# The first MLP's first weight: its scale from TensorE products of its pieces instead of ScalarE squares, with a new stored sequence

## The chip, the core and the metric

The kernel runs on one core of one Trainium2 chip. The metric is device time in microseconds (us), lower is better. The core has five engines that run their own instruction queues side by side: TensorE (PE, matmuls; the loading of its stationary operand is listed apart as PEld), VectorE (DVE), ScalarE (ACT), GpSimd (POOL) and SyncE (SP, which here only issues DMAs). The tile framework makes an engine wait, by semaphores, where one instruction needs another's result or its buffer.

## What is computed

Windowed attention (4 batches, 8 heads, 576 positions, head size 64; plain windows for four heads and dilated ones for the other four), then two MLPs over the 2304 tokens. Cut to what matters:

```python
def _attn_ref(q, k, v):                      # 4 x 8 x 576 x 64
    scores = scale * np.matmul(q, k.transpose(0, 1, 3, 2))
    scores = np.where(masks[None], scores, -1000000000.0)   # window 32, or 32 steps of 4
    attn = softmax(scores)
    return np.matmul(attn, v)

def _moe_ref(x, w_in, w_out, g_ln):          # w_in 512 x 1024, w_out 1024 x 512
    h = x @ w_in
    solu = h * softmax(h)
    return (layernorm(solu) * g_ln) @ w_out

def _moe2_ref(x, w_in, w_out):               # 512 x 2048, 2048 x 512
    return softplus(x @ w_in) @ w_out
```

The large products are made in float16, each operand split into a high and a low half that are both scaled by a power of two. The scale of a weight is found on the chip, from the weight itself. The weights arrive as 8-byte floats.

## The kernel before

All work is cut into some 2900 named operations (`P.op`), each with one to a few dozen instructions. `Plan.order` (L92) does not decide anything: it walks the tuple `ORDER` (L191), which names the operations by their numbers in the sequence in which all engines get them, and takes each buffer from the slot that `SLOTS` names. A number above the count of operations means that DVE does an operation which ACT could do too. A negative number is a fill: a matmul of the 128x128 identity with four copies of itself, 512 columns, into a PSUM bank that is free just then; its result is never read. So the order on every engine is fixed beforehand, and every engine executes its own list strictly in that order.

`weights` (L708) prepares one weight. It is called for `w1i` (the first MLP's first weight, 8 pieces of 128x512), `w1o` (8 pieces), and for each quarter `w2i0` to `w2i3` and `w2o0` to `w2o3` of the second MLP's weights (4 pieces each). Per piece it makes:

- `w1i.3l`: the DMA that loads piece 3 (512 KB) into a raw buffer, of which there are four
- `w1i.3ca`, `cb`, `cc`: three DVE instructions that turn 8-byte floats into 4-byte ones
- `w1i.3s`: a Square on ACT over the 128x512 piece, with the sum of each row kept in a column of `amw`; the squares themselves are written over the raw buffer and never read
- after the squares of all pieces `w1im`, a product with a matrix of ones that sums `amw` over the partitions, and `w1iea` to `w1ied`, four small DVE instructions that make of the sum the power of two by which the weight is scaled
- `w1i.3h` and `w1i.3o`: the float16 high half (ACT or DVE) and low half (DVE)

The names of other operations: `pre0.6`, `pre0.6s` and `pre0m` (loads of a batch's q, k or v, their squares on ACT, the sum); for the pair of attention blocks `n`: `ldN` (loads), `tqN`/`tkN` (transposes on PE), `cqN`/`ckN` (copies out of PSUM), `QKN` (scores), `exN.0a`/`b` (largest entry on DVE, exponentials on ACT), `tpN`, `cpN` (the exponentials turned and copied), `PVN` (values), `nrN` (division), `txN`, `xhN`, `xlN` (the turned result and its two halves); from pair 10 on float16 pairs with `mx`, `ph`, `pl` and transposing DMAs `qT`, `kT`, `pT`. For tile `t` of 128 tokens `m1at`, `m1bt` are the products with `w1i`, and `m1mt` to `m1lt` its softmax and normalisation; `yaJ`, `ybJ` are the products with `w1o`, `hJ.p` and `oJ.p` those of the second MLP, `ghJ.p` and `glJ.p` its halves.

In the first third of the run all weights are prepared while attention and the first tiles go on; from some 237 us on the weights are done and PE works through the MLPs.

`weights` has a second way for the row sums, under the tuple `GRAM` of weight names (L186). It is empty in this kernel.

Of the kernel before, what the change touches and what calls it, by code (L numbers as in the profile page):

```python
# [13 lines left out]
ALU = mybir.AluOpType  # L14
AXX = mybir.AxisListType.X
# [129 lines left out]
def kernel(  # L145
# [12 lines left out]
    nc = tc.nc  # L158
# [27 lines left out]
    GRAM = ()  # L186
# [5 lines left out]
        64, 65, 237, -2, 240, 3166, 238, 268, -2, 242, 3168, -2, -2, 244, 245, 256, 267, 0, 270, 13, 14, 271, 257,  # L192
        3, 15, -2, -2, 272, 4, 66, 5, 67, 246, 16, -2, -2, -2, -2, -2, 247, 3173, 68, 6, 258, 69, -5, 70, 239, 273,
        -5, 274, 71, 72, 73, 74, 75, 269, 259, 275, 17, 1, 28, 7, 29, 286, 276, -5, 249, 298, 30, -5, -5, -5, -5,
        277, 2, 278, 250, 287, 18, 297, -5, -5, -5, -5, 303, 31, 304, 32, 260, 251, 288, 19, 3177, 253, 254, 20,
        21, 22, 261, 299, 300, 305, 306, 3214, 262, 33, -5, -5, -5, 279, 3188, 264, 255, 265, 280, 281, 34, 38,
        266, 35, 307, 308, 36, 282, 355, 283, 309, 290, 291, 23, 39, 292, -5, -5, -5, -5, -5, -5, 310, 40, 37, 284,
        24, 354, 41, 8, 25, 285, 26, 9, 353, 293, -5, -5, -5, -5, -5, 294, 311, 42, -5, 360, 352, 10, 11, 27, 295,
        296, 361, 319, 76, 12, 77, 301, 356, -5, -5, -5, -5, -5, -5, -5, -5, -5, -5, -5, -5, -5, -5, 43, 44, 45,
        46, 47, 358, 302, 320, 407, 91, -5, -5, -5, 321, 359, 408, 111, 78, 50, 362, 52, 2985, 322, 79, 62, 80, 53,  # L200
        363, 364, 312, 410, 437, 411, 313, 61, 374, 48, 92, 314, -5, -5, -5, -5, -5, -5, 365, 63, 323, 366, 3240,
        324, 49, 81, 93, 51, 375, -5, -5, -5, 316, 58, 412, 413, -5, 376, 377, 325, 357, 94, 106, 409, -5, -5, -5,
        -5, 414, 317, 326, 56, 95, 327, 328, 318, 59, 112, 415, 57, 113, 438, 329, 367, 107, 368, 114, 369, 416,
        54, 55, -5, -5, -5, -5, -5, -5, 417, 491, 1128, 418, -5, 440, 108, 426, 441, -5, 419, 96, 378, 109, 82,
        420, 379, 330, 83, 115, 380, 370, 371, 427, 492, 97, 110, 138, 84, 381, 372, 85, 428, 331, 98, 86, 489,
        373, 382, 99, 101, 429, 490, 100, 87, 421, 139, 442, 443, 422, 88, 332, 430, 431, 383, 89, 90, 102, 385,
        432, 333, 103, 384, 104, 227, 140, 545, 544, 439, 423, 497, 334, 495, 424, 335, 105, 496, 228, 172, 425,
        336, 433, 498, 141, 337, 142, 143, 386, 444, 149, 434, 467, 338, 339, 387, 211, 445, 154, 456, 435, 494,
        173, 340, 446, 174, 436, 848, 447, 175, 457, 341, 116, 150, 448, 342, 549, 176, 117, 144, 343, 847, 151,
        118, 344, 388, 119, 345, 152, 458, 547, 459, 346, 548, 449, 120, 450, 155, 550, 212, 347, 213, 493, 499,  # L210
        153, 156, 348, 500, 501, 157, 158, 451, -3, -3, -3, -3, -3, -3, -3, -3, -3, -3, 502, 121, 511, 512, 460,
        513, 503, 514, 850, 851, 3274, 3377, 350, 461, 145, 453, 462, 3047, 146, 454, 504, 463, 214, 852, 505, 464,
        455, 853, 225, 506, 3057, 3432, 147, 3049, 133, 177, -2, -2, -2, -2, 508, 226, 178, 148, 465, 466, 125,
        509, 510, 877, -4, -4, -4, -4, -4, -4, 159, 134, 126, 389, 878, 515, 516, 179, 517, 160, 3443, 180, 161,
        215, 551, 390, 552, 162, 392, 136, 216, 217, 163, 123, 553, -2, 519, 181, 182, 391, 563, 130, 520, 183, -2,
        -2, -2, -2, -2, -2, -2, -2, -2, 554, 521, 128, 555, 135, 468, 218, 522, 131, 564, 351, 219, 393, 184, 523,
        883, 129, 394, 137, 185, 395, 220, 186, 170, 565, 187, 164, 188, 880, 221, 546, 222, 127, 396, 189, 879,
        397, 190, 191, 566, 884, 398, 223, 171, 469, 574, 166, 224, 885, 399, 192, 849, 579, 854, 1129, 193, 229,
        165, 194, 400, 195, 168, 1124, 167, 401, 196, 230, 402, 1127, 886, 231, 169, 232, 855, 233, 403, 575, 234,
        576, 404, 235, 197, 577, 198, 866, -4, -4, -4, -4, -4, -4, -4, -4, -4, -4, 556, 470, 557, 405, 199, 1126,  # L220
        856, -4, 857, 578, 567, 568, 867, 580, 868, 558, 858, 859, 471, 569, 589, 559, 560, 581, 200, 860, 472,
        474, 473, 582, 869, 861, 406, 870, 1136, 201, 1137, 871, 590, 570, -5, -5, -5, 571, 475, 583, 202, 572,
        862, 591, 872, 573, 592, 524, 882, 584, -5, -5, -5, -5, 863, 203, 207, 204, 208, 593, 607, 864, 865, 585,
        205, 873, 938, 874, 881, 1170, 209, 875, 206, 586, 561, 562, 587, 476, 210, 477, 876, 939, 478, 608, 588,
        940, 479, 941, 609, 480, 1177, 610, -5, -5, 594, 481, 887, 888, 595, 482, 612, 596, 236, 483, 611, 597,
        484, 1178, 598, 889, 899, 613, 3524, 485, 900, 614, 617, 486, 3528, 615, 934, 525, 487, 935, 936, 890, 937,
        1125, 901, 616, 891, -5, -5, -5, -5, -5, 892, 618, 902, 601, 893, 903, 912, 619, 605, 1130, 942, 622, 894,
        895, 896, 602, 904, 1134, 620, 600, 621, 1132, 488, 526, 1131, 1133, 687, 623, 905, 624, 625, 1135, 1139,
        897, 898, 527, 1138, 606, 528, 626, 529, 943, 947, -5, -5, -5, 627, 628, 629, 682, 3869, 530, 630, 913,
        906, 631, 531, 1168, 945, 632, 633, 604, 634, 532, 910, 948, 635, 1169, 533, 907, 636, 908, 534, 637, 949,  # L230
        535, 1211, 644, 911, 909, 536, 640, 642, 638, 537, 914, 954, 959, 538, 645, 539, 915, 950, 639, 641, 643,
        540, 541, 542, 955, 688, 1171, 683, 689, 1140, 1172, 946, 690, 916, 1141, 684, 1142, 1175, 691, 1176, 1173,
        685, 917, 956, 543, 951, 919, 918, 672, 1154, 1143, 1209, 1180, 686, 957, 1174, 677, 1144, 1155, 1145, 920,
        953, 952, 673, 960, 1156, 921, 922, 1179, 674, 678, 675, 923, 679, 924, 1146, 1210, 680, 992, 1050, 1157,
        1051, 676, 1181, 925, 1182, 1212, 1158, 1159, 1214, 1052, 1183, 1213, 926, 710, 681, 961, 993, 994, 705,
        1216, 1195, 692, 693, 962, 694, 1184, 1215, 927, 695, 996, 1160, 696, 1217, 1273, 1220, 699, 1275, 1147,
        697, 1196, 1276, 701, 700, 997, 928, 1148, 1197, 958, 995, 963, 1149, 702, 703, 1185, 704, 1150, 1274,
        1161, 998, 929, 930, 1221, 1151, 698, 999, 1012, 706, 711, 1053, 707, 1222, 1152, 1153, 1198, 931, 1000,
        708, 1186, 932, 712, 709, 1283, 1054, 1162, 713, 714, 1284, 720, 965, 1187, 1013, 1223, 721, 1055, 1163,
        1057, 1056, 722, 1279, 1014, 1001, 1005, 1017, 964, 723, 1199, 715, 1002, 1164, 933, 724, 1006, 1165, 716,  # L240
        1236, 717, 718, 1003, 1058, 1280, 719, 725, 726, 727, 1224, 728, 1200, 775, 729, 1218, 1059, 1007, 730,
        1166, 1281, 731, 1060, 1288, 732, 1061, 733, 4207, 1004, 770, 734, 1062, 1201, 735, 1018, 740, 736, 1237,
        1008, 741, 1238, 1188, 1024, 1063, 742, 738, 1189, 1015, 1190, 739, 4116, 1167, 1287, 1064, 743, 1219,
        1009, 1202, 737, 1065, 1225, 1226, 966, 1239, 1227, 1228, 1278, 1016, 771, 1019, 1010, 776, 1192, 1193,
        1066, 1194, 1203, 1020, 777, 1204, 1067, 1289, 4130, 967, 1229, 1025, 1068, 778, 968, 772, 779, 1290, 969,
        1230, 1206, 1207, 1026, 773, 1291, 1240, 1231, 1069, 1241, 1070, 774, 4157, 1011, 971, 785, 1303, 1304,
        1027, 1021, 972, 786, 1292, 1208, 1023, 1029, 1242, 1233, 973, 780, 1305, 1243, 1234, 974, 1235, 1413,
        1293, 1294, 787, 1244, 781, 1306, 970, 1245, 782, 975, 1277, 1030, 1246, 788, 789, 1247, 1295, 783, 654,
        784, 1022, 1285, 1248, -4, 790, 1031, 1307, 976, 791, 792, 793, 1251, 977, 794, 795, 1286, 1308, 801, 796,
        1249, 1296, 1032, 1297, 799, 800, 655, 1298, 797, 802, 803, 798, 804, 1299, 1300, 805, 1250, 1309, 808,  # L250
# [457 lines left out]
    def weights(name, parts, fbufs, am, extra=None, sq_scale=None, after=(), wait=(), kind=None):  # L708

        squares, loads, fs = [], [], []  # L710
        n = len(parts)
        gram = Buf(ps_q) if name in GRAM else None
        for i, (src, _, _) in enumerate(parts):
            raw = Buf(wraw_pool)
            ld = P.op(
# [1205 lines left out]
```

## Time and profile before

| | us |
|---|---|
| three runs, median (lowest to highest) | 683.8 (683.12 to 684.52) |
| the run that was profiled, its own time | 685.53 |
| its span, first to last instruction | 683.6 |
| PE busy | 663.3 |
| DVE busy | 612.5 |
| ACT busy | 499.9 |

The profile is of one execution. Its span is what all positions in time below are counted in; some 1.9 us of its own time lie outside the span. Busy times count every instruction of the engine, for PE the fills among them; a fill is no work that the result needs, so a busy PE in a stretch with fills means a waiting one.

### The profile page before, as it was taken

The numbers are of one execution on the slowest core, as the hardware profiler recorded it, in microseconds if no ns is written. First come the engines' busy times: TensorE is split into PE (matmuls) and PEld (weight loads), VectorE is DVE, ScalarE is ACT, GpSimd is POOL, SyncE is SP. The second block draws the span as 40 slices with busy tenths as digits, with TensorE's granted clock in tenths as the row PEclk, the third lists the DMA queues.
The fourth block names the chain that finished last, engine by engine and source line by source line (L and its number), as shares of the span: only waits on it lengthen the run. The fifth ranks groups of instructions, "written<-read, shape, count | busy, mean of one in ns | idle before, by whom it ended". The sixth has DMA issues, their size and how long they took to land.

```text
span 683.6 us, 14817 instructions
## 1 busy us (share of the span) xinstructions
PE 663.3 (97%) x5437; PEld 482.2 (71%) x5437; DVE 612.5 (90%) x1753; ACT 499.9 (73%) x1051; POOL 3.5 (1%) x22
## 2 busy tenths in 40 slices
PE   6999988999999999999999999999999999999997
PEld 4665546766775587777666758765858786888886
DVE  4999989999999878797888899977998999999997
ACT  4898988999999669987898789755743543545462
POOL 2000000000000000000000000000000000000000
PEclk9999999999999999999999999999999999999999
DMA  9999988779766669898668878853112200000000
GB/s 266 265 246 252 235 236 174 172 170 189 156 136 166 177 176 222 181 193 164 139 141 151 157 127 172 138 98 65 32 32 47 48 1 1 32 1 1 33 32 31
DMA packets 187063, 89.83 MB, mean 131 GB/s; under 512 B 157032, under 2 KB 174960, under 8 KB 186992
## 3 DMA queue, kind: packets, MB, share of 16 engines
q1 hardware_dynamic: 186992, 88.90, 57.9%
q8 instruction: 42, 0.69, 0.5%
q14 instruction: 29, 0.24, 0.1%
HBM read 54.53 MB, written 4.72 MB: 87 GB/s over the span
## 4 chain that ended last, share of the span: by engine, by line
PE 81%; DVE 8%; DMA 5%; ACT 3%; issue 1%; SPq 0%; DVEq 0%; ACTq 0%
PE bank L569 35%; PE ps_w L569 28%; PE bank L1695 11%; PE ps_w L1605 8%; DVE W L560 3%; DMA W<-in_moe_w_out_dram 1%; DMA qT<-qk 1%; PE bank L575 1%; DMA E<-in_k_dram 1%; DMA qk<-in_v_dram 1%; DVE E L560 1%; ACT W L551 1%; DMA pT<-p 1%; DMA rq<-in_q_dram 1%; DVE osb L560 1%
## 5 line engine op out<-in xcount | busy, mean ns | idle before, releaser
L569 PEld LDWEIGHTS <-W 128*128 128x128 f16 x1824 | 177.3, 98 | 23.7 <-DMA lnT<-hl 0.5
L569 PE MATMUL ps_w<-W,g 128*128 128x512 f16 x576 | 130.4, 379 | 0.0
L569 PE MATMUL bank<-y,W 128*128 128x256 f16 x960 | 109.9, 273 | 0.0
L569 PE MATMUL bank<-lnT,W 128*128 128x256 f16 x864 | 98.9, 274 | 0.3 <-DVE W L560 0.3
L569 PEld LDWEIGHTS <-g 128*128 128x128 f16 x576 | 55.4, 98 | 60.3
L569 PE MATMUL ps_w<-W,xr 128*128 128x512 f16 x432 | 97.6, 379 | 0.0
L569 PEld LDWEIGHTS <-xr 128*128 128x128 f16 x432 | 41.6, 99 | 45.4
L1695 PEld LDWEIGHTS <-W 128*128 128x128 f16 x528 | 51.7, 98 | 7.5
L1889 ACT ACT_TABLE_LOAD x39 | 50.0, 1283 | 0.7
L551 ACT ACTIVATE s<-s 96x128 f32<-96x128 f32 (+3 forms) x144 | 43.4, 375 | 4.9 <-DVE s L557 4.1
L551 ACT ACTIVATE E<-E 128x768 f32<-128x768 f32 (+3 forms) x52 | 38.4, 738 | 9.0 <-issue 3.9
L1136 DVE CUSTOM_DVE_ANT_0 s<-bank,band,bsc 96x128 f32<-96x128 f32 (+3 forms) x144 | 38.8, 323 | 2.7 <-PE bank L569 2.3
L560 DVE SCALAR_TENSOR_TENSOR g<-r,KR,g 128x512 f16<-128x512 f32 (+1 forms) x54 | 38.6, 717 | 0.2 <-ACT g L551 0.2
L551 ACT ACTIVATE r<-bank,invC 128x512 f32<-128x512 f32 x40 | 27.0, 684 | 15.1 <-PE bank L569 10.3
L551 ACT ACTIVATE g<-r,KR 128x512 f16<-128x512 f32 (+1 forms) x40 | 27.4, 687 | 7.8 <-PE ps_w L1605 4.8
L551 ACT ACTIVATE hl<-e,st 128x1024 f16<-128x1024 f32 x18 | 22.3, 1237 | 13.8 <-DVE st L560 11.1
L551 ACT ACTIVATE xf<-bank,rs 80x64 f32<-80x64 f32 (+1 forms) x116 | 26.4, 314 | 4.2 <-DVE rs L566 2.7
L569 PEld LDWEIGHTS <-eye 128*128 128x128 bf16 (+2 forms) x160 | 16.4, 108 | 17.6 <-issue 4.3
L560 DVE SCALAR_TENSOR_TENSOR E<-E 128x512 int32<-128x512 int32 x40 | 27.2, 686 | 0.3
L1605 PE MATMUL ps_w<-W,g 128*128 128x256 f16 x180 | 25.9, 273 | 0.7 <-DVE osb L560 0.6
L569 PEld LDWEIGHTS <-pT 128*96 128x96 f16 (+3 forms) x432 | 22.9, 123 | 4.4 <-DMA pT<-p 1.2
L563 DVE TENSOR_TENSOR p<-s,p 96x512 f16<-96x512 f32 (+3 forms) x36 | 21.9, 608 | 4.3 <-ACT p L551 4.1
(360 smaller groups left out, 1316.8 us busy)
## 6 DMA issues: line engine op xcount, KB each, us to landing
E<-in_moe_w_in_dram SPq DMA_DIRECT2D x17, 512.0 KB, 4.5
E<-in_moe_w_out_dram SPq DMA_DIRECT2D x17, 512.0 KB, 3.9
out_dram<-osb SPq DMA_DIRECT2D x16, 256.0 KB, 2.3
W<-in_moe_w_in_dram SPq DMA_DIRECT2D x7, 512.0 KB, 5.9
W<-in_moe_w_out_dram SPq DMA_DIRECT2D x7, 512.0 KB, 5.1
E<-in_v_dram SPq DMA_DIRECT2D x9, 384.0 KB, 4.4
E<-in_q_dram SPq DMA_DIRECT2D x9, 384.0 KB, 3.8
E<-in_k_dram SPq DMA_DIRECT2D x9, 384.0 KB, 4.0
```

The lines of the kernel that those rows point to most:

```text
L551: pin(nc.scalar.activation(out=out, in_=in_, func=func, **kw))
L560: pin(nc.vector.scalar_tensor_tensor(out=out, in0=in0, scalar=s, in1=in1, op0=op0, op1=op1, **kw))
L563: pin(nc.vector.tensor_tensor(out=out, in0=a, in1=b, op=op))
L569: pin(nc.tensor.matmul(out, l, r, start=start, stop=stop))
L575: pin(nc.tensor.transpose(out, in_, eye32[:in_.shape[0], :in_.shape[0]]))
L1136: pin(nc.vector.tensor_tensor_reduce(out=sv()[:rows, h, :nk], in0=sb.t[:rows, h, :nk], in1=band[:rows, 48 - m:48 - m + nk], scale=sc[:rows ...
L1605: pin(nc.tensor.matmul(mi[q](), gt.t[:, a, ff, 128 - 128 * t:256 - 128 * t], b(w), start=start and x == 0, stop=x == 2, skip_group_check=True,
L1695: pin(nc.tensor.matmul(ps.t[:, ff, :], at(w, cc, ff), yo.t[:, v, cc, :], start=start, stop=cc == 1 and x == 2, skip_group_check=True,))
L1889: pin(nc.scalar.preload_act_table_set(TABLES[tab]))
```

## The change

`GRAM` names `w1i`. For this weight the eight Squares on ACT fall away. For each piece, PE multiplies the upper 16 bits of its 4-byte floats, read as bfloat16 (every second 2-byte element), with themselves: four products of 128x128 by 128 columns, all 32 summed in one 128x128 block of PSUM. The block lies in a `ps_w` buffer (two of them, two banks each) and no longer in one of the four `bank`s. Then one new DVE operation, `w1ix`, takes the largest entry of each row of the block into the one column of `amw` that `w1im` sums. The code of the products is mended in one point (`n=n`, so that the last product and not another one closes the sum).

```diff
-    GRAM = ()
+    GRAM = ("w1i",)
...
-        gram = Buf(ps_q) if name in GRAM else None
+        gram = Buf(ps_w) if name in GRAM else None
...
-            def products(e, fb=fb, fo=fo, i=i):
+            def products(e, fb=fb, fo=fo, i=i, n=n):
                 x = fb.t[:, fo:fo + 512].bitcast(BF16).rearrange("p (n t) -> p n t", t=2)[:, :, 1]
                 for c in range(4):
                     t = x[:, 128 * c:128 * c + 128]
-                    mm(gram.t[:, 0:128], t, t, i == c == 0, i == n - 1 and c == 3)
+                    mm(gram.t[:, 0, 0:128], t, t, i == c == 0, i == n - 1 and c == 3)
...
-                f"{name}x", dve_cost(128, x=1), lambda e: pin(nc.vector.tensor_reduce(out=am[:, 0:1], in_=gram.t[:, 0:128], axis=AXX, op=ALU.max)),
+                f"{name}x", dve_cost(128, x=1), lambda e: pin(nc.vector.tensor_reduce(out=am[:, 0:1], in_=gram.t[:, 0, 0:128], axis=AXX, op=ALU.max)),
...
-    ORDER = (64, 65, 237, -2, 240, 3166, 238, 268, -2, 242, 3168, -2, -2, 244, ...
+    ORDER = (the new sequence, 3070 entries for 3065)
-    SLOTS = (0, 0, 0, 0, 0, 1, 1, ...
+    SLOTS = (the new slots, 1125 entries for 1124)
```

The two tuples are new from the first entry to the last. Put back into names they say the following. (A sequence below lists all engines' operations as stored; `x8` is a count of fills.)

The first operations before and after:

```
before: pre0.6 pre0.6s ld0.0 fill tq0 cq0 ld0.1 ld1.1 fill tk0 ck0 fill x2 QK0 ex0.0a ex0.1a ld1.0 ... w1i.2l w1i.2ca
after:  ld0.0 ld0.1 fill tk0 ck0 tq0 cq0 fill x2 QK0 ex0.0a ex0.1a pre0.6 w1i.0l pre0.6s w1i.0ca w1i.0cb
DVE after, from there: w1i.0cc w1i.2ca w1i.2cb ck1 pre0ea ... pre0ed w1i.2cc ex1.0a ex1.1a w1i.5ca
PE after, from QK0:    QK0 tq1 fill x8 tp0.0 tk1 tp0.1 pre0m fill x2 QK1
```

The end of the row sums of `w1i`:

```
before, DVE: w1i.1ca w1i.1cb w1i.1cc xl1.1 ex2.1a w1o.0ca w1iea w1ieb w1iec w1ied w1o.0cb
before, PE:  tk3 fill x14 w1im tq3 fill x3 tp2.1 QK3
after, DVE:  w1i.1ca w1i.1cb w1i.1cc w1i.4cc xl1.1 ex2.1a ck3 w1o.0ca w1ix w1o.0cb w1iea w1ieb w1iec w1ied
after, PE:   tp2.0 fill x9 tk3 tx1.1 fill x3 w1i.1s w1i.2s ... w1i.7s tp2.1 tq3 tq4 w1im fill x2 QK3
```

Fills on PE, between operations that stand in the same sequence in both (in all 140 before, 144 after):

| from, to | before | after |
|---|---|---|
| start, `w1im` | 51 | 43 |
| `w1im`, `m1a0` | 25 | 27 |
| `m1a0`, `m1b3` | 30 | 19 |
| `m1b3`, `w2o0m` | 0 | 5 |
| `w2o0m`, `PV7.0` | 10 | 9 |
| `PV7.0`, `tx7.0` | 1 | 13 |
| `tx7.0`, `ya0.1` | 7 | 12 |
| `ya0.1`, end | 16 | 16 |

Engines: 111 operations, apart from the nine of the row sums, change between ACT and DVE, some in either direction. Of those that ran in the first 237 us these are all: `ck0`, `cp0.0` and `cp1.1` go from DVE to ACT, `ck1`, `ck3` and `gT` (a copy of 8 columns) from ACT to DVE. DMAs are the same 345 in number and size, in another sequence.

## Rows read from the trace of the kernel before

**Rows 1.** The page's busy us, share of the span, instructions

```profile
PE 663.3 (97%) x5437; PEld 482.2 (71%) x5437; DVE 612.5 (90%) x1753; ACT 499.9 (73%) x1051; POOL 3.5 (1%) x22
```

**Rows 2.** Busy us by stage: length, PE, PEld, DVE, ACT, POOL, clock, DMA, GB/s

```profile
0.00:16.20 16.20, 10.56 (x76) 6.66 (x76) 6.37 (x17) 7.76 (x22) 3.52 (x22) 1.00 0.96 265
16.20:56.50 40.30, 40.27 (x323) 26.66 (x323) 39.73 (x98) 35.80 (x118) 0.00 (x0) 1.00 0.95 251
56.50:158.00 101.50, 93.24 (x695) 60.96 (x693) 96.82 (x288) 94.74 (x241) 0.00 (x0) 0.97 0.86 204
158.00:237.00 79.00, 78.91 (x617) 52.93 (x618) 74.52 (x227) 71.28 (x148) 0.00 (x0) 1.00 0.71 168
237.00:683.60 446.60, 440.36 (x3732) 334.94 (x3729) 395.11 (x1125) 290.36 (x529) 0.00 (x0) 1.00 0.45 93
```

**Rows 3.** Groups of PE instructions, the fills: busy us, mean ns, idle before

```profile
L569 PE MATMUL ps_w<-eye 128*128 128x512 bf16 x82 | 22.2, 390 | 0.0
L569 PE MATMUL bank<-eye 128*128 128x512 bf16 x58 | 18.1, 439 | 4.8 <-POOL eye L627 4.0 <-ACT kT L551 0.7 <-DVE rs L566 0.2
```

**Rows 4.** Timeline at the last Squares: start, us, engine, instruction [idle before <-releaser]

```profile
27.77 0.60 PE L575 MATMUL bank<-eye,W 128*128 128x128 f32 x4
...
28.20 3.19 PE L569 MATMUL ps_w<-eye 128*128 128x512 bf16 x14
...
30.37 0.47 DVE L563 TENSOR_TENSOR xr<-bank,xr 128x144 f16<-128x144 f32 x1
30.48 0.63 ACT L551 ACTIVATE W<-W 128x512 bf16<-128x512 f32 x1 [0.25 <-DVE W L560]
...
30.64 0.65 DVE L1027 TENSOR_REDUCE s<-bank 96x4 f32<-96x512 f32 x1
...
31.22 0.41 DVE L557 TENSOR_SCALAR W<-E 128x512 int32<-128x512 int32 x1
31.26 0.39 PE L569 MATMUL bank<-amw,ones 128*128 128x8 f32 x2
...
31.69 0.17 DVE L751 TENSOR_REDUCE s1i<-bank 128x1 f32<-128x8 f32 x1
```

**Rows 5.** Timeline of PE, 140 to 150 us: eight float16 products of 128 columns

```profile
142.70 0.61 PE L569 MATMUL bank<-kT,qT 128*96 128x128 f16 x8
143.15 5.34 PE L569 MATMUL ps_w<-W,g 128*128 128x512 f16 x24
```

**Rows 6.** Timeline of DVE, 6 to 16 us: its waits at the start

```profile
9.93 0.88 DVE L1027 TENSOR_REDUCE s<-bank 80x4 f32<-80x320 f32 x2 [2.18 <-PE bank L569]
...
14.20 0.49 DVE L587 COPY pT<-bank 80x320 f32<-80x320 f32 x1 [0.67 <-PE bank L575]
```

**Rows 7.** Timeline of PE, 90 to 113 us, and DVE's wait in it

```profile
93.26 0.63 PE L575 MATMUL bank<-eye,rk 128*128 128x128 f32 x4 [1.54 <-DMA rk<-in_k_dram]
...
96.92 3.97 PE L569 MATMUL bank<-eye 128*128 128x512 bf16 x10 [0.70 <-ACT kT L551]
...
105.02 0.36 PE L575 MATMUL bank<-eye,xf 80*128 80x80 f32 x2 [1.68 <-ACT xf L551]
...
101.49 0.22 DVE L557 TENSOR_SCALAR rs<-bank,bsc 80x4 f32<-80x4 f32 x1 [1.30 <-PE bank L569]
```

**Rows 8.** Busy time and clock in two stretches; columns as in rows 2

```profile
96.90:100.30 3.40, 3.38 (x9) 1.14 (x9) 3.29 (x13) 3.37 (x7) 0.00 (x0) 0.50 0.94 251
107.10:110.50 3.40, 3.14 (x14) 1.53 (x12) 3.40 (x11) 3.40 (x15) 0.00 (x0) 0.50 1.18 259
```

**Rows 9.** Timeline of DVE, 226 to 240 us: the last weight's scale

```profile
233.71 0.16 DVE L751 TENSOR_REDUCE s2o<-bank 128x1 f32<-128x4 f32 x1 [1.73 <-PE bank L569]
```

**Rows 10.** Busy time late in the run, and PE's two waits after 237 us

```profile
340.00:400.00 60.00, 60.00 (x518) 40.78 (x519) 53.17 (x201) 51.07 (x111) 0.00 (x0) 1.00 0.80 148
...
340.00 0.65 PE L569 MATMUL bank<-v,pT 112*80 112x65 f16 x12 [0.74 <-DMA pT<-p]
...
661.68 0.49 PE L1605 MATMUL ps_w<-W,g 128*128 128x256 f16 x3 [0.62 <-DVE osb L560]
```

## What the change should do to the time

> **What bounds the kernel now.** I read four views in this order. First the page's busy times [rows 1]: PE is busy for 97% of the span, but 140 of its matmuls are fills [rows 3], 0.216 us each (fourteen in a row take 3.19 us, the last one's own 0.38 in it: 2.81 / 13 [rows 4]), some 30 us in all. So a busy PE does not mean a PE that bounds. Second the busy time by stage [rows 2]. Until 237 us DVE has hardly a gap: it is idle for 9.8 us before 16.2, then for 0.6 of 40.3, for 4.7 of 101.5 and for 4.5 of 79.0. ACT is idle for 8.4, 4.5, 6.8 and 7.7 us in the same stages. PE waits or makes fills: 134 of the 140 stand ahead of 158 us. From 237 us on it turns round: PE is busy for 440.4 of 446.6 us, with no fill. Of the other 6.2 us two waits ahead of its end make 1.4 (0.74 and 0.62 [rows 10]); most of the rest lies at the very end, in the last evictions and the last store.
>
> So the time is the moment at which the last weight is ready (237 us, set by DVE's list) and then PE's own work (446.6 us), which the change leaves alone. A gain can only come from DVE: less work in its list, or less of the 19.6 us that it is idle until then. Third and fourth, the timelines at the end of the eight Squares [rows 4] and around DVE's longest waits [rows 6, 7, 9] say what these idle times are: waits for PE, not for ACT.
>
> **Removed: eight Squares on ACT.** The last one starts at 30.48 us and takes 0.63, and the product of its sum starts at 31.26 [rows 4], so one holds ACT for 0.63 to 0.78 us; eight at the lower end, where the next instruction follows at once, are 5.2 us with a little for each readout. ACT waits for DVE's conversion just before the last one (0.25 us [rows 4]): it has nothing queued up there. In the stage that holds the Squares ACT is idle for 4.5 us and DVE for 0.6 [rows 2]. So what is taken off ACT makes ACT's gaps longer. It could help DVE only where DVE waits for ACT, which is in those 0.6 us at most. I take 0; bounds -0.6 and 0.
>
> **Added: 32 products on PE.** Eight float16 products of 128 columns, each with its own stationary operand, are followed by the next matmul after 0.45 us, 0.056 each [rows 5]: 1.8 us for 32. Four float32 transposes of 128x128 take 0.43 us to the next matmul, 0.108 each [rows 4]: 3.4 us. The new ones are 16-bit and so nearer to the first; that they read every second element no row shows, so both stay bounds. With four more fills PE gets 2.7 us more (1.8 + 4 x 0.216). The cover is PE's waiting until 158 us, 43 us of it (134 fills x 0.216 = 28.9, and 13.9 not busy [rows 2]), so the cost is 0. Without the cover it would be the 1.8 to 3.4.
>
> **Added: one maximum on DVE, 128 columns.** Between 0.17 us (8 columns) and 0.65 (512 columns) [rows 4], along the line between them 0.3. It stands in the engine that sets the time, so it counts in full. Beside it come `gT` (0.17, like the small one) and two copies `ck1` and `ck3`, and three copies of 0.49 [rows 6] go to ACT. I summed DVE's durations along both sequences, an operation that keeps its engine with its own duration and a moved one with its kind's median: ahead of `h0.6`, the first product that needs the last weight, they are 216.3 us before and 216.4 after. The cost is +0.1, bounds 0 and +0.5. The same sum for ACT falls by 4.1 us.
>
> **The wait for the products.** In the new list DVE comes to `w1ix` after `w1o.0ca`, and everything behind it, all of DVE's conversions, waits if PE is late. PE has `w1i.1s` to `w1i.7s` in one go after `tk3`, `tx1.1` and three fills, and `w1i.4s` needs DVE's `w1i.4cc`. DVE has `xl1.1` (0.47), `ex2.1a` (0.65), `ck3` (a copy like the 0.49 in rows 6) and `w1o.0ca` (0.41 [rows 4]) between `w1i.4cc` and `w1ix`, about 2.0 us. PE has four pieces' products there, 0.9 to 1.7 us. So they are covered, by 0.3 to 1.1 us. Then `w1im` stands behind two groups of transposes and DVE has `w1o.0cb` (0.68) meanwhile, against 0.43 from `w1im` to `w1iea` before [rows 4]: about 0.3 us may be left over. I take +0.2; bounds 0 and +1.5. The Trainium skill ("TensorE: Matmul & The Clock Gate", the table at its head) says that ScalarE and VectorE take their instructions strictly first in, first out, and that only TensorE pulls weight loads ahead. The trace agrees: DVE stood still for 0.67 us ahead of a copy out of PSUM [rows 6], with the conversion `w1i.0cc` next behind it.
>
> **Moved: the start.** `ld0.0` and `ld0.1` go ahead of `pre0.6`'s load, so `QK0` comes earlier and DVE's 2.18 us wait [rows 6] gets shorter. But DVE then comes to `ck1` sooner, which needs `tk1`, and on PE that stands behind eight fills and `tp0.0`. Before, DVE had done 4.6 us of work when the copy that waits for `tp0.0` ended, at 14.7; after, it has 4.5 ahead of the end of `ck1`, which cannot be much earlier. I take 0; bounds -0.7 (no more than the next wait, 0.67 [rows 6], can be kept) and +1.1 (`pre0ea` has 5.7 us of DVE's work ahead of it before and 4.6 after, and the rest must wait behind it).
>
> **Moved: 91 to 112 us.** Here PE waits for a load (1.54 us), for ACT (0.70, 1.68) and DVE loses 1.30 us to PE [rows 7]. The granted clock is 0.50, the lower of its two levels (1.2 GHz), from 96.9 to 100.3 and again from 107.1 to 110.5 [rows 8], after PE's waits; ten fills take 3.97 us there [rows 7], where fourteen took 3.19 [rows 4]. The ten fills end after what `PV7.0` waits for, and that is DVE's 1.30 us. The new sequence has 39 fills for 18 between `m1b3` and `ya0.1`, and 11 fewer ahead of it. That may keep the clock up and save the 1.30; or the fills themselves end late. I take half, -0.7; bounds -1.3 and +1.0 (thirteen fills for one ahead of `tx7.0`, 2.6 us, less the 1.68 of waiting that they replace). The Trainium skill (the same page, "Part 1: The HAM clock gate") says that the half clock is the default and that activity lifts it. By that rule the new fills save the whole 1.3, a forecast of 683.2 in place of 683.8; the trace has the two drops after PE's gaps, on its side.
>
> **Moved: after 237 us.** PE is the bound and idles for only those 1.4 us ahead of its end; the longer wait, 0.74 us, is for a transposing DMA [rows 10]. A new sequence can hardly win here, and it can lose. DVE's list there carries 1 to 4 us more than before ahead of the same operations between 340 and 420 us. I take +0.6, most of one such wait; bounds -1.4 and +4.
>
> **The sum.** 0 + 0 + 0.1 + 0.2 + 0 - 0.7 + 0.6 = +0.2 us on a span of 683.6. The profiled run's own time was 685.53, 1.9 above its span and 1.7 above the median of the runs shown, so I put the change on the median, 683.8, and leave out the 0.2, which is far inside the bounds: **683.8 us**, no change. A measurement of this kernel tells about 0.2% (1.4 us) from none: the same means 682.4 to 685.2.
>
> **The rivals.** *The new sequence closes DVE's gaps.* After 56.5 us DVE is idle for 9.2 us until 237 [rows 2], 1.30 and 1.73 of them in two single waits for PE [rows 7, 9]. ACT is 4.1 us ahead in its list, so what hangs on ACT and then PE comes sooner. If a third is closed, the time falls by 3.1, to 680.7; if half, to 679.2. For it speaks that PE stands between ACT and DVE in most of these waits; against it that ACT has gaps of its own, in which a lead of 4 us is lost by 56.5. *DVE's halves come late for PE between 340 and 420 us.* In the new list DVE does 1.3 to 3.6 us more ahead of `pl18.0` to `pl22.1`, the low halves whose transposes `PV18.0` to `PV22.1` wait for. `PV18.0` already waits for its own [rows 10], so there is little margin. The point from which it decides: DVE is idle for 6.8 of the 60 us from 340 to 400 [rows 10], and if that does not swallow the extra, each of about five waits costs PE 0.7 us, like the one in the row: +3.5, 687.3. Against it: ACT's list is 10 us lighter there. *The change does not do what it is for in the scale chain*: the products take twice their time, `w1ix` holds DVE up by 1 to 1.5 us, 685.1, inside the forecast's own range.
>
> **How the numbers follow.** No change 0.40 (with the third rival's 0.06 in it); faster 0.33, of which 0.28 by the first rival and 0.05 by the clock, where it comes with the lower bounds of the other terms; slower, by the second rival or by waits of the new sequence elsewhere, 0.27. The range takes in both rivals with half of DVE's gaps closed on one side and the second rival's price on the other: 679.2 to 688.0. The likeliest case's own range is 682.4 to 685.2.
>
> **What would show it.** ACT's busy time falls to about 496 and PE gets 36 matmuls more, 32 of 128x128 bf16. `s1i`'s first reduction starts at 31.5 to 33.5 us. DVE is busy for over 39 of the 40.3 us from 16.2 on, and the first product of the last quarter (at 237 us now) starts within 1.5 us of that. The clock stays at 1.00 between 91 and 112 us if the fills do as the rule says. The forecast is wrong if that first product moves by more than 1.5 us (then DVE's idle time moved: look for which waits), or if PE has more than 2 us of waits after 237 us (then the second rival).

## The result and the profile after

The changed kernel took 692.9 us, the kernel before 683.85 beside it: 1.0129 times as long, 95% interval 1.0105 to 1.0153. It is slower by 9.1 us, where no change was forecast and 688.0 was the upper end of the range. The profiled run has an own time of 694.15 and a span of 692.3.

The page's busy times, and the busy time by stage (length, PE, PEld, DVE, ACT, POOL, clock, DMA, GB/s), which answer to [rows 1, 2]:

```profile
PE 667.9 (96%) x5473; PEld 484.5 (70%) x5473; DVE 614.0 (89%) x1755; ACT 495.7 (72%) x1043; POOL 3.5 (1%) x22
```

```profile
0.00:16.20 16.20, 8.39 (x56) 5.57 (x57) 4.51 (x10) 7.33 (x19) 3.52 (x22) 0.94 0.90 260
16.20:56.50 40.30, 39.25 (x332) 26.34 (x331) 36.47 (x94) 27.62 (x89) 0.00 (x0) 0.94 0.83 222
56.50:158.00 101.50, 95.45 (x724) 63.55 (x723) 97.08 (x280) 94.45 (x245) 0.00 (x0) 0.98 0.84 203
158.00:237.00 79.00, 78.03 (x608) 51.63 (x607) 75.92 (x228) 73.28 (x152) 0.00 (x0) 1.00 0.79 171
237.00:692.30 455.30, 446.73 (x3760) 337.44 (x3758) 399.98 (x1147) 293.07 (x543) 0.00 (x0) 1.00 0.48 94
```

The work is as forecast: ACT 495.7 us busy, 36 more matmuls on PE. What is lost is order. Ahead of 56.5 us DVE is busy for 41.0 us and was for 46.1 [rows 2], and ACT, which lost the Squares, has not become an engine that pulls ahead: it stands idle longer. The start of the same operation in the two traces says where the loss comes in (us; the lower rows belong to the experiments):

| kernel | `w1iea` | `m1a0` | `h0.0` | `QK11.0` | `h0.6` | `PV14.0` | `PV18.0` | `PV22.1` | span |
|---|---|---|---|---|---|---|---|---|---|
| before | 31.7 | 46.5 | 125.9 | 158.1 | 236.8 | 281.9 | 340.0 | 402.2 | 683.6 |
| changed | 37.7 | 51.9 | 131.4 | 162.4 | 242.5 | 289.0 | 347.1 | 408.9 | 692.3 |
| e1, old sequence, with products | 32.9 | 47.8 | 125.0 | 156.1 | 234.7 | 280.4 | 337.6 | 399.8 | 681.1 |
| e12, e1 with the new start | 37.9 | 52.9 | 130.8 | 161.7 | 240.4 | 286.0 | 343.6 | 405.9 | 687.0 |
| e8, changed, start mended | 34.6 | 48.8 | 126.4 | 157.1 | 237.6 | 283.9 | 341.9 | 402.5 | 686.1 |
| e5, old to 215 us, new rest | 33.2 | 48.1 | 125.9 | 156.8 | 236.3 | 282.9 | 341.2 | 402.5 | 686.2 |
| e10, new to 215 us, old rest | 35.8 | 50.0 | 130.3 | 161.2 | 243.7 | 288.9 | 346.2 | 408.4 | 689.6 |

So the changed kernel is 5.4 us late at `m1a0` and still 5.7 late at `h0.6`: those are lost in the first 50 us. PE's waits behind that, below, come to 3.6 us against 0.7. 5.7 and 2.9 make 8.6 of the 8.7 us by which the span grew.

That is an account of one execution of each kernel. e10 has the changed kernel's order up to 215 us and e3 up to some 290, and in their profiled runs `m1a0` starts at 50.0 and 50.1, so 3.5 us late and not 5.4. And the kernel before is not the only measure: against e1, the old order with the products, the changed kernel is 4.1 us late at `m1a0` and 7.8 at `h0.6`. The 3.7 us between are a third loss, which does not show against the kernel before (190.3 us from `m1a0` to `h0.6` there, 190.6 in the changed kernel, 186.9 in e1).

**The start.** SP's issues (SPq: start, us to the end of the last issue in the row, with any wait between two issues in it), before:

```profile
3.68 0.82 SPq L578 DMA_DIRECT2D E<-in_moe_w_in_dram  x2
4.91 1.30 SPq L578 DMA_DIRECT2D W<-in_v_dram  x2
```

and after:

```profile
2.26 0.43 SPq L578 DMA_DIRECT2D E<-in_moe_w_in_dram  x1
...
4.04 3.33 SPq L578 DMA_DIRECT2D W<-in_v_dram  x2
7.41 0.43 SPq L578 DMA_DIRECT2D E<-in_moe_w_in_dram  x1
```

The two loads of v are `pre0.7` and `pre0.8`, those of `in_moe_w_in` are `w1i.2l` and `w1i.0l`. `pre0.8` uses the buffer of `pre0.6`, so its issue waits until ACT has squared that (`pre0.6s`). Before, `pre0.6` was the very first load and both weight pieces were ahead of the wait; now `pre0.6` is third, the wait lasts to 7.0 us (2.5 of the 3.33 us lie between the two issues), and `w1i.2l` stands behind it. What that does, in the timeline of the changed kernel (start, us, engine, instruction, [idle before <-releaser]):

```profile
9.93 1.89 PE L569 MATMUL bank<-eye 128*128 128x512 bf16 x8
...
12.20 0.84 ACT L551 ACTIVATE W<-W 128x768 f32<-128x768 f32 x1 [0.78 <-DMA W<-in_v_dram]
...
13.04 0.95 ACT L551 ACTIVATE s<-bank,s 80x80 f32<-80x80 f32 x4
...
14.04 0.58 PE L575 MATMUL bank<-eye,s 80*80 80x80 f32 x4 [2.22 <-ACT s L551]
14.41 0.74 PE L575 MATMUL bank<-eye,W 80*128 80x80 f32 x4
...
14.91 0.43 DVE L557 TENSOR_SCALAR W<-E 128x512 int32<-128x512 int32 x1 [4.16 <-DMA E<-in_moe_w_in_dram]
...
15.98 0.48 DVE L587 COPY kT<-bank 128x320 f32<-128x320 f32 x1
...
18.79 0.88 DVE L1027 TENSOR_REDUCE s<-bank 80x4 f32<-80x320 f32 x2 [1.09 <-PE bank L569]
```

The kernel before had the same two steps, DVE's `w1i.2ca` and PE's `tk1`, without a wait:

```profile
10.73 0.41 DVE L557 TENSOR_SCALAR W<-E 128x512 int32<-128x512 int32 x1
...
11.27 0.58 PE L575 MATMUL bank<-eye,W 80*128 80x80 f32 x4
```

There are two chains. DVE stands 4.16 us before `w1i.2ca` for the load, with its whole list behind (1.71 in e10 and 2.24 in e3, where the load is issued at 7.38 and 7.15: the issue is as late in all three, the landing is not). Beside it ACT's list has `pre0.8s` (12.20, the late load) ahead of `ex0.0b` (13.04), for which PE waits 2.22 us before `tp0.0`; `tk1` (14.41) stands behind that, `ck1` (DVE, 15.98) needs `tk1`, and `QK1` needs `ck1`. PE's gaps of 1.63 and 2.22 us are followed by the lower level of its clock (0.50, 1.2 GHz), in which it makes `QK1` and the fills behind:

```profile
15.50:21.00 5.50, 5.50 (x33) 3.09 (x32) 4.27 (x13) 1.67 (x7) 0.00 (x0) 0.50 0.82 134
```

**The end of the row sums**, which answers to [rows 4]:

```profile
33.64 1.78 PE L569 MATMUL ps_w<-W 128*128 128x128 bf16 x28
...
35.88 0.28 DVE L742 TENSOR_REDUCE amw<-ps_w 128x1 f32<-128x128 f32 x1
...
36.30 0.55 PE L575 MATMUL bank<-eye,s 96*128 96x96 f32 x4 [0.89 <-ACT s L551]
...
37.30 0.32 PE L569 MATMUL bank<-amw,ones 128*128 128x1 f32 x2
...
37.66 0.16 DVE L751 TENSOR_REDUCE s1i<-bank 128x1 f32<-128x1 f32 x1 [0.90 <-PE bank L569]
```

28 products take 1.78 us and the reduction 0.28, without a wait ahead of it. `w1iea` waits 0.90, since `w1im` stands behind `tp2.1` in PE's list, and that waits 0.89 for ACT.

**Behind 237 us.** PE's waits in the changed kernel from 242 to 430 us (what it waited for: us, times, longest), which answer to PE's one wait of 0.74 in [rows 10]:

```profile
PE bank L569 <- DMA pT<-p: 3.2, 4, 1.0
PE bank L569 <- DMA qT<-qk: 0.4, 1, 0.4
```

The four are `PV14.0`, `PV15.0`, `PV19.0` and `PV22.1`. Around `PV15.0`:

```profile
294.68 0.48 DVE L563 TENSOR_TENSOR p<-s,p 80x320 f16<-80x320 f32 x1
294.75 1.86 SPq L581 DMA_TRANSPOSE kT<-qk  x1
...
296.67 1.16 SPq L578 DMA_DIRECT2D rk<-in_k_dram  x2
297.99 1.21 SPq L581 DMA_TRANSPOSE pT<-p  x1
...
302.37 0.65 PE L569 MATMUL bank<-v,pT 80*80 80x65 f16 x12 [1.02 <-DMA pT<-p]
```

DVE's low half `pl15.0` is done at 295.16, but the transpose is issued 2.8 us later: SP has `kT16` and two loads ahead of it.

### The profile page after: what moved, and what is told of

Same layout as the page of the kernel before. It is cut to its first block, busy times and chain, and to the rows that moved or that the text cites. A ratio compares the mean times of both kernels' runs of the same rounds, so it can differ in the third digit from the quotient of the medians.

```text
span 692.3 us, 14885 instructions
## 1 busy us (share of the span) xinstructions
PE 667.9 (96%) x5473; PEld 484.5 (70%) x5473; DVE 614.0 (89%) x1755; ACT 495.7 (72%) x1043; POOL 3.5 (1%) x22
## 4 chain that ended last, share of the span: by engine, by line
PE 70%; DMA 9%; DVE 9%; ACT 8%; issue 2%; SPq 1%; ACTq 0%; DVEq 0%
PE bank L569 27%; PE ps_w L569 25%; PE bank L1695 10%; PE ps_w L1605 7%; DMA pT<-p 4%; DMA W<-in_moe_w_in_dram 2%; DVE W L560 1%; DMA W<-in_v_dram 1%; PE bank L575 1%; ACT s L551 1%; ACT E L551 1%; ACT xf L551 1%; ACT e L551 1%; DMA E<-in_v_dram 1%; DVE osb L560 1%
## 5 line engine op out<-in xcount | busy, mean ns | idle before, releaser
L569 PEld LDWEIGHTS <-W 128*128 128x128 f16 (+1 forms) x1856 | 178.8, 98 | 24.7 <-issue 0.7
L569 PE MATMUL ps_w<-W,g 128*128 128x512 f16 x576 | 130.7, 379 | 0.0
L569 PE MATMUL bank<-y,W 128*128 128x256 f16 x960 | 110.2, 273 | 0.1
L569 PE MATMUL bank<-lnT,W 128*128 128x256 f16 x864 | 98.9, 273 | 0.1
L569 PE MATMUL ps_w<-W,xr 128*128 128x512 f16 x432 | 98.5, 379 | 0.0
L569 PEld LDWEIGHTS <-g 128*128 128x128 f16 x576 | 55.4, 98 | 59.8
L569 PEld LDWEIGHTS <-xr 128*128 128x128 f16 x432 | 41.5, 99 | 44.6
L1695 PEld LDWEIGHTS <-W 128*128 128x128 f16 x528 | 51.7, 98 | 7.0
L560 DVE SCALAR_TENSOR_TENSOR g<-r,KR,g 128x512 f16<-128x512 f32 (+1 forms) x53 | 37.9, 716 | 0.2
L551 ACT ACTIVATE xf<-bank,rs 80x64 f32<-80x64 f32 (+1 forms) x128 | 29.4, 319 | 8.4 <-DVE rs L566 5.7
L569 PEld LDWEIGHTS <-eye 128*128 128x128 bf16 (+2 forms) x164 | 16.6, 108 | 19.0 <-issue 5.1
L569 PEld LDWEIGHTS <-pT 128*96 128x96 f16 (+3 forms) x432 | 22.5, 123 | 7.3 <-DMA pT<-p 4.2
L569 PE MATMUL bank<-v,pT 128*96 128x65 f16 (+3 forms) x432 | 23.5, 206 | 3.2 <-DMA pT<-p 3.2
L551 ACT ACTIVATE g<-r,KR 128x512 f16<-128x512 f32 (+1 forms) x36 | 24.7, 689 | 2.5 <-PE ps_w L1605 1.2
```

The costliest lines, as they stand in the source:

```text
L551: pin(nc.scalar.activation(out=out, in_=in_, func=func, **kw))
L560: pin(nc.vector.scalar_tensor_tensor(out=out, in0=in0, scalar=s, in1=in1, op0=op0, op1=op1, **kw))
L569: pin(nc.tensor.matmul(out, l, r, start=start, stop=stop))
L1695: pin(nc.tensor.matmul(ps.t[:, ff, :], at(w, cc, ff), yo.t[:, v, cc, :], start=start, stop=cc == 1 and x == 2, skip_group_check=True,))
```

## The experiments

All but e2 have the products in. An order is changed by moving names in the stored sequence, and a diff below shows only the names that move on one engine's list. In the kernels' lines L564 is the L569 above, and so on: the tuples differ in length. "Ratio" is to the kernel before on the same chip, with the 95% interval.

**e1, the change without the new sequence.**

```diff
 (the sequence before, GRAM = ("w1i",))
-ACT: w1i.0s ... w1i.7s
+PE:  gt w1i.0s fill ...  tk3 fill x10 w1i.1s ... w1i.7s tq3 w1im
-DVE: w1o.0ca w1iea w1ieb w1iec w1ied w1o.0cb w1i.6h w1o.0cc
+DVE: w1o.0ca w1o.0cb w1ix w1o.0cc w1iea w1ieb w1iec w1ied w1i.6h
-ACT: cq3 w1i.1h w1i.2h cp2.1
+ACT: cq3 cp2.1 w1i.1h w1i.2h
```

> The old sequence, to which only the new way of summing the squares of w1_in is added: 32 products on TensorE (piece 0's ahead of the first PV, the other seven right behind w1i.1cc), the largest-entry reduction on VectorE behind w1o.0cb, fills of the other half of ps_w in between; three VectorE steps and one ScalarE step nearby change places so that nothing stands idle behind the scale. Theory S (the loss is the new sequence's, the sums themselves cost nothing): 683.8, within 0.8 either way; ScalarE about 4 us less busy, VectorE 0.3 more, VectorE no longer idle before w1iea than 0.3 us. Theory G (the products and the longer way to the scale cost the time): at least 687, up to 693, with a gap of VectorE before w1iea and m1's first half late.

682.84 us, ratio 0.9980 (0.9964 to 0.9996): as theory S had it, and faster than before by what can just be told from none. ACT is busy for 495.8 us. The products, in its timeline:

```profile
30.23 1.79 PE L564 MATMUL ps_w<-W 128*128 128x128 bf16 x28
...
32.05 0.29 DVE L737 TENSOR_REDUCE amw<-ps_w 128x1 f32<-128x128 f32 x1
...
32.86 0.15 DVE L746 TENSOR_REDUCE s1i<-bank 128x1 f32<-128x1 f32 x1
```

Neither reduction shows a wait. `w1iea` is 1.2 us later than in the kernel before and `m1a0` 1.3, but `h0.0` is 0.8 us earlier. So the same 28 products, the same reduction and the same small chain that stand in the changed kernel cost nothing here that reaches the end: theory G falls, and the whole loss is the sequence's.

**e2, the new sequence without the change.**

```diff
-    GRAM = ("w1i",)
+    GRAM = ()
-PE:  w1i.0s ... w1i.7s      DVE: w1ix
+ACT: w1i.Ns right behind w1i.Ncc, for N of 0 to 7
```

> The new sequence, with the eight squares of w1_in on ScalarE as before (each right behind its conversion), no products and no largest-entry reduction. Theory S: the start still waits 4.2 us for w1i.2l and the late transposes still stand behind others on SP's queue: 691.5 (690 to 692.9), w1iea 1.5 to 2.5 us earlier than 37.7, as the products are gone. Theory G: 684 to 686.

701.15 us, ratio 1.0235 (1.0204 to 1.0266): a miss of both theories. ACT's waits in its first 57 us show why:

```profile
ACT E L546 <- DVE W L555: 9.9, 4, 4.7
```

These are Squares that wait in ACT's list for their conversion, with the exponentials queued behind them. As a measure of the sequence alone the run is spoiled by the places that I gave the Squares.

**e4 and e6, halves joined at 60 and 70 us.**

```diff
 e4: the order of e1 for the steps that the new sequence has up to 60 us, then the new one
 e6: the new order for the steps that e1 has up to 70 us, then that of e1
```

> With the products in. The steps that the new sequence has in its first 60 us stand in the order of the old one (that of e1_products_old_sequence); everything behind stands as in the new sequence. Theory S, two places: the start gives back its 5.7 us and the 3.3 us behind 270 us stay: 687.2 (686 to 688.5). If the late loss only follows from the late start: 683.8. If the start's loss is made up or lost again further on, 691 or more.

> With the products in. The mirror of e4_old_start_new_rest: the first 70 us or so in the new sequence's order, everything behind in the old one's (as in e1_products_old_sequence, 682.8). Theory A (each stretch costs by itself; the gap of VectorE for w1i.2l sets the end): 682.8 + 4.5 to 5.5 = 687.3 to 688.5. Theory B (a late start is made up later, since the stretch behind it has a bound of its own, as e4 gained only 1.1 us): 683.5 to 685. TensorE's shift against e1's trace at 60, 160 and 240 us shows where.

e4 took 691.84 us (1.0112, 1.0074 to 1.0150), e6 693.89 (1.0139, 1.0110 to 1.0167), so each half seems to cost the whole; e6 is a miss of both its theories. Both have a wait right behind their seam that is much smaller in both parents (1.2 us in the changed kernel, 0.5 in e1, from 57 to 100 us): DVE's waits in e4 from 57 to 100 us, and in e6 from 60 to 100:

```profile
DVE E L552 <- DMA W<-in_moe_w_out_dram: 3.0, 2, 2.3
```

```profile
DVE E L552 <- DMA W<-in_moe_w_out_dram: 5.1, 2, 4.0
```

I read it so that a seam there breaks the agreement between the sequence of loads and that of the conversions; no run shows that by itself. These two are no measure of either half; I joined later halves at 215 us, where one step differs between the two sides.

**e5 and e10, halves joined at 215 us.**

```diff
 e5:  the order of e1 up to xl12.1 (about 215 us), then the new one
 e10: the new order up to there, then that of e1
```

> With the products in. The old order up to about 215 us (step xl12.1), the new sequence behind. Theory S, two places: 683.8 + 3.3 = 687.1 (686 to 688.5), with TensorE waiting about 3 us for pT behind 240 us. If the late loss only follows from the late start: 683.8 within 0.8.

> With the products in. The complement of e5_old_to_215us_new_rest: the new sequence's order up to about 215 us, the old one's behind, with a seam at which only one step of each stands on the other side. If the late loss belongs to the order behind 215 us and adds to the rest: the waits for pT before PV14.0, PV15.0, PV19.0 and PV22.1 go and the time is 692.9 - 4 = 689 (688 to 690). If it follows from what comes before: 692 to 693, with the waits still there.

e5 took 687.76 us (1.0050, 1.0032 to 1.0068), e10 689.75 (1.0078, 1.0055 to 1.0102), both inside what the theory of two places gave. PE's waits from 236 to 425 us in e5:

```profile
PE bank L564 <- DMA pT<-p: 3.5, 4, 1.2
```

They are before `PV14.0`, `PV15.0`, `PV19.0` and `PV22.1` again, 1.2 us at most. In e10 the same view has no row at all. So these waits belong to the order behind 215 us whatever came before: 0.70% against e1, 0.51% against the changed kernel, 3.5 to 4.8 us.

**e3, four steps moved behind the late transposes.**

```diff
-SP: kT16 ld17.10 ld17.11 pT15.0     SP: ld20.21 pT19.0     SP: lnT10 pT22.0
+SP: kT16 pT15.0 ld17.10 ld17.11     SP: pT19.0 ld20.21     SP: pT22.0 lnT10
```

> The changed kernel, with four steps of SP's queue moved behind a transpose that TensorE waits for: ld17.10 and ld17.11 behind pT15.0, ld20.21 behind pT19.0, lnT10 behind pT22.0. Theory L (the late loss is these transposes, standing behind others on SP): the waits of 1.02, 0.99 and 0.92 us before PV15.0, PV19.0 and PV22.1 go, 690.2 (689.7 to 691). Rival: the transposes then collide with the loads in flight, or VectorE's steps before them are the late ones, and the waits stay: 692 to 693.

693.82 us (1.0139, 1.0108 to 1.0170): no gain, and above what either theory gave. The waits before `PV15.0` and `PV19.0` are gone, but those before `PV14.0` (1.3), `PV15.1` (0.7) and `PV22.1` (2.1) grew. `PV14.0` comes ahead of the first step that moved, so its 1.3 us, 0.26 in the changed kernel, are a difference between two executions and not the edit's. SP around the last one:

```profile
398.66 1.21 SPq L576 DMA_TRANSPOSE pT<-p  x1
399.93 2.82 SPq L576 DMA_TRANSPOSE lnT<-hl  x1
402.80 1.69 SPq L576 DMA_TRANSPOSE xd<-E  x1
404.53 1.52 SPq L576 DMA_TRANSPOSE qT<-E  x1
406.48 1.55 SPq L576 DMA_TRANSPOSE pT<-p  x1
```

`pT22.0` went out 1.6 us earlier, and DVE had the next half ready at 403.8, but then `lnT10`, `xT21.0` and `qT24` held SP until after 406. SP takes 1.2 to 2.8 us for a transpose; one that is let pass pushes the others back. That the late place is SP's list holds for `PV15.0` and `PV19.0`. The repair as a whole failed, and only the exchange of the whole order in e10 shows what it is worth.

**e7, one load first.**

```diff
-SP: pre0.7 pre0.8 w1i.2l
+SP: w1i.2l pre0.7 pre0.8
```

> The changed kernel, with one step moved: the load w1i.2l stands ahead of pre0.7 and pre0.8 on SP's queue instead of behind them, so it is issued at 4.0 us and not at 7.4. Theory A: VectorE's 4.2 us at 10.7 shrink to less than 1, but ck1, which waits for tk1 at 15.2, and QK1 at half the clock then hold VectorE for 1.5 to 2.5: 690.5 to 691.5. If that one load were the whole of the start's loss: 687.5. Theory B (made up later): 692 to 693, with the shift gone by 160 us.

694.15 us (1.0137, 1.0098 to 1.0175): no gain, and above all three forecasts. DVE's waits in the first 57 us:

```profile
DVE kT L582 <- PE bank L570: 4.1, 1, 4.1
...
DVE W L552 <- DMA E<-in_moe_w_in_dram: 0.6, 1, 0.6
```

The 4.2 us for the load became 0.6, and the second chain took its place: `pre0.8` landed later (ACT's `pre0.8s` at 13.70 instead of 12.20), so `ex0.0b`, `tp0.0`, `tk1` and `ck1` came later. The longest wait in the profile was worth nothing by itself, since another was hidden under it. I had put this second wait at 1.5 to 2.5.

**e8, the start mended on three queues.**

```diff
-SP:  ld0.0 ld0.1 pre0.6 w1i.0l gl ld1.0 ld1.1 pre0.7 pre0.8 w1i.2l
+SP:  pre0.6 ld0.0 ld0.1 w1i.0l gl ld1.0 ld1.1 w1i.2l pre0.7 pre0.8
-ACT: ex0.1b pre0.8s ex0.0b pre0.7s
+ACT: ex0.1b ex0.0b pre0.7s pre0.8s
-PE:  tq1 fill x8 tp0.0 tk1
+PE:  tq1 fill x2 tk1 fill x6 tp0.0      (and one fill fewer ahead of tx6.1)
```

> The changed kernel, with the first 16 us repaired on every queue at once: on SP pre0.6 first and w1i.2l ahead of pre0.7 and pre0.8; on ScalarE ex0.0b and pre0.7s ahead of pre0.8s; on TensorE tk1 ahead of tp0.0, two fills behind tq1; on VectorE ck1 behind w1i.2cb. Theory A (the start's loss is a wait on each of several queues, and reaches the end once all are mended): VectorE's waits before w1i.2ca and ck1 together under 1.5 us, TensorE's shift against the kernel before falls from 5.5 to 2 or 3 at 60 us, and 689 to 690 at the end. Theory B (the stretch from 60 to 160 us takes the time up anyway): shift gone by 160 us, 692 to 693.

689.57 us (1.0087, 1.0063 to 1.0112), 0.42% or 2.9 us less than the changed kernel. DVE's list needed no edit: `ck1` stands behind `w1i.2cb` in the changed kernel already. Its DVE timeline has no wait ahead of `w1i.2ca` (12.86) or of `ck1` (13.93), where there were 4.16 us; but DVE's first wait, for PE's `tq0`, is 6.5 us long and was 4.6:

```profile
12.86 0.42 DVE L552 TENSOR_SCALAR W<-E 128x512 int32<-128x512 int32 x1
13.31 0.69 DVE L555 SCALAR_TENSOR_TENSOR W<-E,W 128x512 int32<-128x512 int32 x1
13.93 0.48 DVE L582 COPY kT<-bank 128x320 f32<-128x320 f32 x1
15.21 0.16 DVE L671 TENSOR_REDUCE tmp<-bank 128x1 f32<-128x3 f32 x1 [0.80 <-PE bank L564]
```

**e12, the start spoiled in the old sequence.**

```diff
-SP:  pre0.6 ld0.0 ld0.1 ld1.1 ld1.0 gl w1i.2l w1i.0l pre0.7 pre0.8
+SP:  ld0.0 ld0.1 pre0.6 w1i.0l gl ld1.0 ld1.1 pre0.7 pre0.8 w1i.2l
-DVE: w1i.2ca w1i.2cb w1i.0ca w1i.0cb w1i.2cc cp0.0 w1i.0cc
+DVE: w1i.0ca w1i.0cb w1i.0cc w1i.2ca w1i.2cb w1i.2cc cp0.0
-ACT: pre0.7s ex0.0b pre0.8s      PE: tk1 fill x5 tp0.0
+ACT: pre0.8s ex0.0b pre0.7s      PE: fill x5 tp0.0 tk1
```

> The mirror of e8_start_reordered: e1_products_old_sequence (682.8), in which only the steps of the first 16 us take the new sequence's places: on SP ld0.0 and ld0.1 first, pre0.7 and pre0.8 ahead of w1i.2l; on VectorE w1i.0 ahead of w1i.2; on ScalarE pre0.8s ahead of ex0.0b and pre0.7s behind it; on TensorE tk1 behind tp0.0. If the start's loss is these places on the queues: 682.8 + 3 = 685.8 (684.8 to 687.8), with VectorE waiting 2 to 4 us for w1i.2l. If the stretch behind takes it up: 683 to 684.

688.17 us (1.0058, 1.0034 to 1.0082), 0.78% or 5.3 us more than e1, and above the 684.8 to 687.8 that I gave. In the table above it is 5.1 us behind e1 at `m1a0` and 5.9 at the end: nothing behind takes it up. DVE's wait for `w1i.2l` is back:

```profile
DVE W L552 <- DMA E<-in_moe_w_in_dram: 3.1, 1, 3.1
```

With e8 this shows the start's loss from both sides: 2.9 us when it is mended in the new order, 5.3 when it is made in the old one.

**e11 and e13, start and end mended together.**

```diff
 e11: the order of e8 up to about 215 us, then that of e1
 e13: e11, with the other of the two raw buffers for w2o3.0 to w2o3.3 and four batch loads
```

> The two repairs that each gave something, together: the mended first 16 us of e8_start_reordered, the new sequence's order from there to about 215 us, the old order behind as in e10_new_to_215us_old_rest. If start and tail are separate losses that add: 692.9 - 3.4 - 3.2 = 686.3 (685.3 to 687.3), which leaves 3.5 us against e1_products_old_sequence for the new order between 16 and 215 us. If both repairs return the same time: 689.5.

> e11_start_mended_old_tail, in which the eight raw buffers of w2o3.0 to w2o3.3 and of four batch loads behind the seam take the other of their two slots. In e11 the load w2o3.0l had to wait on SP, from 217.8 to 222.5 us, for the slot of pre2.4, which the new order had put there: a cost of the seam. If that is why e11 came out 1.6 us over the sum of the two repairs: 686 (685.2 to 687), and VectorE no longer waits 2.1 us for E at 226. If start and tail overlap instead: 687.9.

e11 took 687.86 us (1.0062, 1.0041 to 1.0082), above the 685.3 to 687.3 that I gave, e13 686.97 (1.0052, 1.0030 to 1.0074), inside its range. The buffer clash that I had found at e11's seam is gone in e13 (`w2o3.0l` is issued 1.3 us behind the step ahead of it, no longer 4.7). The sum of the two repairs was 1.0036 and lies inside e13's interval, so the losses may well add; the intervals are too wide to say it of the last microsecond. e13 still stands 0.7%, 5 us, above e1. About 1 us of it is there at `m1a0` in the profiled runs (48.9 in e13, 47.8 in e1); the rest is the new order from there to 215 us, and a part of that may not be the order at all: e8, e11 and e13 have the same sequence up to 215 us, and from `m1a0` to `h0.0` the profiled runs took 77.5, 80.8 and 80.5 us. (These three executions took 687.87, 690.26 and 690.24 us, where the medians of the kernels are 689.57, 687.86 and 686.97.) The four other profiled runs with this order (the changed kernel, e3, e7, e10) took 79.4 to 81.1 us there, those with the old one and the products (e1, e5, e12) 77.2 to 78.0. So some 2 us seem to belong to the order, and two executions of one order differ by more. The clock of 100 to 130 us in e8 and in e11:

```profile
100.00:130.00 30.00, 28.80 (x255) 22.20 (x253) 29.92 (x87) 27.72 (x81) 0.00 (x0) 1.00 0.69 173
```

```profile
100.00:130.00 30.00, 28.55 (x224) 20.84 (x223) 27.19 (x80) 25.15 (x74) 0.00 (x0) 0.89 0.58 152
```

**i1 and i2, towards something better than e1.**

```diff
 i2 (on e1)
-DVE: w1i.6h w1i.2o ex3.0a nr2.0a w1i.6o ex3.1a w1o.3ca
+DVE: w1i.6h w1i.6o w1o.3ca w1i.2o ex3.0a nr2.0a ex3.1a
 i1 (on i2)
-DVE: cp1.1 nr0.1c
+ACT: cp1.1 nr0.1c
```

> e1_products_old_sequence, with VectorE eased in the start by what ScalarE has free: cp1.1 and nr0.1c on ScalarE (0.9 us), and w1i.6o and w1o.3ca moved up into VectorE's 1.5 us gap before w1i.2o. If VectorE sets the time up to 158 us: 682.8 - 2 = 680.8. If the loads of w1_out and w2 are what comes late next: 682.8, VectorE waiting for E and W by DMA between 55 and 95 us instead.

> e1_products_old_sequence, with only w1i.6o and w1o.3ca moved up into VectorE's 1.5 us gap before w1i.2o (no step changes engines, unlike i1_products_old_sequence_eased). If that gap of VectorE is on the path: 681.8. If i1's 2.7 us of loss came from this move and not from cp1.1 and nr0.1c on ScalarE: 684 to 685.5. If neither: 682.8.

i1 took 685.62 us (1.0018, 1.0003 to 1.0033), a miss of both its theories, i2 684.09 (0.9996, 0.9979 to 1.0014). In i2 the 1.5 us that DVE waits for ACT ahead of `w1i.2o` are 0.3, but 0.8 us of waiting for ACT came up elsewhere, and no time was gained. In i1 two operations went to ACT, which had the time for them, and PE waits 0.42 us ahead of `PV1.0` for `cp1.1`, now on ACT, and DVE 1.4 ahead of `nr1.0a` for `PV1.0`. i2 lies 0.16% above e1 and i1 0.22% above i2, each within the noise of such a difference (some 0.24%); that i1 lies above e1, by 0.38%, is clear. e1 has the lowest ratio of all kernels here.

## Why the prediction was wrong

- **The Squares, 0: right as far as can be told.** ACT's busy time fell by 4 us (499.9 to 495.8 in e1); e1, in which a few other steps moved as well, is faster by 0.04 to 0.36%, i2 cannot be told from the kernel before, and no gap of DVE that waited for ACT disappeared with them.
- **The 32 products, 1.8 to 3.4 us under cover: right.** 28 take 1.78 with the last one's own time in it, and in e1 the next matmul starts 1.62 after the first of them, 0.058 each, so 32 take 1.9, and cost nothing in e1 that reaches the end. That they read every second element shows next to nothing (0.056 in [rows 5]). **The maximum, 0.3: right**, 0.28.
- **The wait for the products, +0.2 of 0 to 1.5: right as to its kind.** No wait ahead of `w1ix`, 0.9 ahead of `w1iea`. I counted DVE's work behind `w1ix` against `w1im`, but not that `tp2.1`, ahead of `w1im` in PE's list, waits for ACT.
- **The start, 0 of -0.7 to +1.1: this step failed.** It measured 5.4 in the profiled run at `m1a0`, 3.5 in those of e10 and e3, which have the same order there, and 2.9 (e8) to 5.3 (e12) in the times. I followed DVE's list to `ck1` and PE's to `tk1`, and took the loads as given. Two things were left out, both to be read in the sequence: `pre0.8`'s issue waits for a buffer that ACT frees, and holds up everything behind it on SP, and `w1i.2l` had come to stand behind it; and ACT's list has `pre0.8s` ahead of the exponential on which `tp0.0`, `tk1` and `ck1` hang. The bound of +1.1 was worked out from DVE's own work, not from the landing of what it reads.
- **91 to 112 us, -0.7: not shown, and where it came true it was luck in part.** In the profiled run of the changed kernel the clock stays at 1.00 there, where it was 0.50 twice [rows 8], and the lag of PE's steps against the kernel before falls from 6.3 us (the middle one of those that lay between 80 and 100 us) to 5.5 at `h0.0`. Its row from 97 to 118 us, where the same work lies now:

```profile
97.00:118.00 21.00, 17.61 (x140) 11.39 (x141) 20.41 (x65) 19.83 (x60) 0.00 (x0) 1.00 0.89 206
```

  But in the same run the clock was at 0.50, the lower level, for 3.4 us from 82.5 on, where the kernel before had 1.00. And of the six other profiled runs with this order (three of them with one fill fewer) only e8's keeps 1.00 between 90 and 130 us: in e3, e7, e10, e11 and e13 it is at 0.50 for 3.4 to 6.8 us, in e11 for instance here:

```profile
107.00:111.00 4.00, 4.00 (x19) 2.56 (x18) 2.73 (x11) 2.27 (x9) 0.00 (x0) 0.50 1.16 210
```

  The Trainium skill's rule ("TensorE: Matmul & The Clock Gate", "Part 1: The HAM clock gate"), by which activity lifts the clock from its default of half, spoke for the new fills keeping it up; the traces of the changed kernel and of e8 agree with that between 97 and 118 us, the five others do not.

- **Behind 237 us, +0.6 of -1.4 to +4: mis-sized, at or above its upper bound.** It measured 3.0 from `h0.6` to the end of the profiled runs, 2.9 of it in PE's waits, and 3.5 to 4.8 by e10 and e5. The second rival had the right place, waits of PE for the transposes of the low halves, and nearly the price (+3.5). It had the wrong cause: for `PV15.0` and `PV19.0` DVE was not late, SP's list was.
- **The first rival** (DVE's gaps behind 56.5 us close) did not come in the changed kernel: from `m1a0` to `h0.6` DVE was idle for 9.8 us, before for 9.2, and ahead of 56.5 for 15.5 instead of 10.4. But the profiled runs with the products in the old order have 5.8 (e1) to 7.9 us (i2) in that part, and e1 takes it in 186.9 us instead of 190.3. So with the products in, such gaps did get smaller in the old order (one execution each; what closed them no run shows), and the new order did not get that.
- The signs that I had named told it at once: `w1iea` at 37.7 and not 31.5 to 33.5, DVE busy for 36.5 of the 40.3 us, `h0.6` 5.7 us later, and over 2 us of PE's waits behind 237 us.

Not settled: of the new order between 16 and 215 us, how much of the up to 5 us that e13 is above e1 is order and how much the clock (no term of the prediction stands for it); and which moves in the list of SP would free the four transposes without holding up others.

## What to carry to other kernels

When a sequence is searched anew, walk the DMA queue's list as closely as the engines': for every load, what its issue waits for (a buffer, and the engine that frees it), and which engine stands at its head when it lands. Of several waits that begin in the same place the longest is not the price: one load moved gave nothing, three lists mended gave 3 us. And separate the edit from the sequence that comes with it first; here the edit without the new sequence was worth 0.2% at best, and the sequence cost 1.5%. And take a second trace of the same order before a number is read off one: here the start of one and the same order differed by almost 2 us.

## What was not expected of the hardware

- An issue that waits for its buffer stops the whole queue: two loads took SP 3.33 us, and the load behind, issued 3.7 us later than before, was read 4.2 us later (2.5 and 2.6 in e10 and e3, issued 3.7 and 3.5 us later).
- SP is held for 1.2 to 2.8 us by each transposing DMA, one after the other, so in this part of the run SP is itself a queue with little room.
- The same instructions in the same sequence ran with different granted clocks: from `m1a0` to `h0.0` in 77.5 us (1.00 between 100 and 130 us, e8) or 80.8 (0.89, e11). The times of single runs of e12 lie between 684.1 and 690.8 us.
